# A fused attention and two-layer MLP kernel: a weight load moved, a gate pair put first in the operand work, and result buffers placed first in their pool

## The chip, the cores and the metric

The kernel runs on one core of one Trainium2 chip. The metric is the device time of one execution in microseconds; the kernel before has a median of 1094.09 us over three runs. TensorE is called PE below, its weight loads PEld, VectorE DVE, ScalarE ACT, GpSimd POOL, and SyncE, which issues nearly all transfers, SP.

## The reference, cut to what matters

Three stages follow each other, all in float32. Chunked attention (windows of 32 queries, 16 left and 8 right neighbours, 8 memory keys) gives x of 3072 tokens by 512. Layer one is gated, layer two is a SiLU layer:

```
scores = scale * np.matmul(q_c, k_full.transpose(0, 1, 3, 2))
a = np.exp(scores - max);  a = a / (sum(a) + 1e-09)
x = a @ v_full                                  # 3072 x 512
x = (sigmoid(x @ w_gate) * (x @ w_val)) @ w_out   # d_ff 1536
h = x @ w_in                                    # d_ff 2048
out = (h * sigmoid(h)) @ w_out2
```

The inputs are float64 on the host and arrive as pairs of 32-bit words, so each weight is first rebuilt (`rebias` on ACT, `join` on DVE) and split into a high and a low part (`high` on ACT, `rest` on DVE). A product is then three matmuls: high by high, high by low, low by high.

## The kernel before, in words

**Prologue.** The first 512 tokens (four tiles, 0 to 3) go through attention before any layer work can start. The order of that work on all engines is written out by hand in the string `PROLOGUE` (L38): each word is a step and a tile or a weight unit. `sc`, `max`, `sub`, `exp`, `sum`, `nm` make the probabilities of a tile, `pt` transposes them on PE and copies them to SBUF on ACT, `px` multiplies by the values, `tr` transposes the result on DVE. `rebias.1`, `join.1`, `high.0`, `rest.0` are steps of weight units 0 (gate columns 0) and 1 (value columns 0). `idle` and `short` are filler matmuls on PE. `load.4` issues the weight loads up to unit 4; the first transfer that this call issues waits for the exp of tile 3 (`behind`, L507). Loads issued before it are those of L472 to L484: queries and keys, then values, with gate unit 0 ahead of the last value tile and, by `feed1.load(2)` at L484, value unit 1 at the end. SP issues transfers strictly in this order.

**Layer one.** Four blocks of 512 tokens (block one to four) run directly: for each of 12 column tiles f, PE computes gate (`pg`) and value (`pv`), ACT the sigmoid (`sg`), DVE the product, and PE the output product `y` of the f before. Attention of later tiles is laid between (`run_events`, L601): `sx` on PE reads `at`, the copy of the transposed probabilities that ACT makes. From block two on, a planner (`Pace`, L803) spends the spare DVE and ACT time on operand work: it forms sums of weight quarters, for the products of the last third of layer one (`PairC`, kinds g, v and o) and of layer two (`Pair2`, two 128-column units of the raw weight `in_w2i_dram`, loaded by SP into `stg_w2i`). The list `items` (L1274 to L1277) gives its order: pair 0 of layer two's first weight, then gate pair 0 and value pair 0, and so on. The constructor of `Pace` issues the load of the first `Pair2` and makes the sums `tcg` of the first gate pair on DVE (`ahead`). Results go through five result buffers (`co`) to DRAM; the engines' instruction order is exactly the order in which the planner emits.

**The rest.** The last 1024 tokens of layer one (b = -1) and layer two (b = 0 to 2, 1024 tokens each) use seven products of summed quarters in place of eight (`pair2`, `out2`). During b = -1 and most of b = 0 a second `Pace` prepares the second weight of layer two in the pool `pp` (L1351): tags `stg0` and `stg1` (4 KB per partition each), `f` (8 KB) and four result buffers `co0` to `co3` (4 KB each, stored to `w2o_d`). After pair 5 of b = 0 the planner finishes, `pp` is closed, and the pool `p3` (L1368) takes its place; `g2_of` (L1046) puts the four activation tiles `g3..` of column pairs 6 and 7 there (16 KB). Tags get their addresses in the order in which they are first used, so in the kernel before `co0` to `co3` are the last 16 KB of `pp`, and `p3`'s four tiles lie on them.

Of the kernel before, what the change touches and what calls it, by code (L numbers as in the profile page):

```python
# [10 lines left out]
I32 = mybir.dt.int32  # L11
# [4 lines left out]
P = 128  # L16
# [21 lines left out]
PROLOGUE = """  # L38
idle.1 short.1 half.0 spread.1 hx.0 half.1 short.1 hx.1 sum.0 spread.2 spread.3 sc.1 nm.0 max.1 sub.1 exp.1 sc.2 max.2 sub.2
exp.2 sc.3 sum.1 nm.1 pt.0 max.3 sub.3 exp.3 load.4 qk.4 idle.1 px.0 sum.2 nm.2 pt.1 rebias.0 sum.3 nm.3  # L40
idle.1 px.1 tr.0 pt.2 pt.3 v.4 tr.1 join.0 rebias.1 px.2 tr.2 px.3 idle.1 high.0 tr.3 rest.0 join.1
"""
NP = 0
NRING = 5
# [12 lines left out]
def moe_kernel(ctx: ExitStack, tc: tile.TileContext, qh, kh, vh, wg, wv, wo, w2i, w2o, out):  # L57
# [15 lines left out]
    def w_slot(i, name):  # L73

        return main.tile([P, 2, 2, 512], F32R, tag=f"w{i}", name=name)
# [121 lines left out]
    def att_load_v(t, vb):  # L197
        nc.sync.dma_start(out=vb, in_=vh[t])
        v_t[t] = vb
# [188 lines left out]
    with tc.manual_schedule():  # L388
# [83 lines left out]
        feed1 = Feed(units)  # L472
# [7 lines left out]
        for t in range(n0):  # L480
            if t == n0 - 1:
                feed1.load(LV)
            att_load_v(t, vs[t])
        feed1.load(2)  # L484

        warm = ps_m("warm")
        fill = ident.rearrange("p (o n) -> p o n", o=1).to_broadcast([P, 4, P])
# [494 lines left out]
        for b in range(-1, NB2):  # L982
            base[b] = len(granules)
            if b < 0:
# [4 lines left out]
                for i in ORDER2:  # L989
                    for q in range(NPAIRC // 2):  # L990
                        if i in (S1, S2, S3, S4):
                            outs.append(wco_d[(S1, S2, S3, S4).index(i), q])
                        else:
                            f, c = 4 * q + (i != A11), 256 * (i == A22)
# [8 lines left out]
        def next_granule():  # L1003
            n = loaded[0]
            loaded[0] += 1
            if n >= len(granules):
                return
            w = w_slot(7 + n % NRING, f"wr{n}").rearrange("p a b c -> p (a b c)")
            k, src, *a = granules[n]
            if k == "o" or k == "m":  # L1010
                w = w.rearrange("p (b a m c) -> p b a m c", b=2, a=2, m=2)
                if k == "o":
                    nc.sync.dma_start(out=w.bitcast(F32), in_=src)
                else:
                    for j, part in enumerate(src):
                        nc.sync.dma_start(out=w[:, j].bitcast(F32), in_=part)
            else:
                w = w.rearrange("p (a m c) -> p a m c", a=2, m=4)
                src = wc_d[src[0], src[1]] if k == "c" else w2i_d[src]
                nc.sync.dma_start(  # L1020
                    out=w[:, :, : a[1]].bitcast(F32), in_=src[:, a[0], :, : a[1]]
                )
            ring[n] = w
# [248 lines left out]

        pending, rests = None, []
        items, gv, prep = [], [(k, p) for p in range(NPAIRC) for k in "gv"], None  # L1274
        for n in range(NPAIR):
            items.append(Pair2("i", n, p1))
            items += [PairC(*gv.pop(0)) for _ in range(2 - n % 2)]  # L1277
        seen = {}
        xgen = None
        for bi, n in enumerate(BLOCKS1[:NB1]):  # L1280
# [70 lines left out]
        pp_cm = tc.tile_pool(name="pp", bufs=1, side="right")  # L1351
        pool = pp_cm.__enter__()
        next_granule()
        prep = Pace([Pair2("o", p, pool) for p in range(NPAIR)], ["co0", "co1", "co2", "co3"], 1, 2.8)
        xgen = iter(())
        for b in range(-1, NB2):
# [106 lines left out]
```

## Time and profile before

| What | Value |
|---|---|
| Median of three runs | 1094.09 us (1093.42 to 1096.15) |
| Profiled execution, its own time | 1096.56 us |
| Its span, first to last instruction | 1094.7 us |
| PE busy | 1081.7 us (99% of the span) |
| DVE, ACT, POOL busy | 756.9 us, 531.5 us, 98.8 us |
| Granted TensorE clock | 1.00 |
| Chain that ended last | PE 96%, DMA 2%, ACT 1%, DVE 1% |

The profile's rows give times from the start of the span in microseconds. "Idle before" is the time that an engine stood still ahead of a group of instructions, with an arrow to what ended it. An engine name with a q (SPq) is its sequencer, which issues transfers and waits. "issue" as a releaser means that the engine waited for nothing that the profile shows. Line numbers are those of the kernel before; in the changed kernel everything after L484 stands one line higher.

### The profile page before, as it was taken

The numbers are of one execution on the slowest core, as the hardware profiler recorded it, in microseconds if no ns is written. First come the engines' busy times: TensorE is split into PE (matmuls) and PEld (weight loads), VectorE is DVE, ScalarE is ACT, GpSimd is POOL, SyncE is SP. The second block draws the span as 40 slices with busy tenths as digits, with TensorE's granted clock in tenths as the row PEclk, the third lists the DMA queues.
The fourth block names the chain that finished last, engine by engine and source line by source line (L and its number), as shares of the span: only waits on it lengthen the run. The fifth ranks groups of instructions, "written<-read, shape, count | busy, mean of one in ns | idle before, by whom it ended". The sixth has DMA issues, their size and how long they took to land.

```text
span 1094.7 us, 18989 instructions
## 1 busy us (share of the span) xinstructions
PE 1081.7 (99%) x7584; PEld 887.8 (81%) x7584; DVE 756.9 (69%) x1133; ACT 531.5 (49%) x775; POOL 98.8 (9%) x76
## 2 busy tenths in 40 slices
PE   7999999999999999999999999999999999999998
PEld 4888878888888888888888888788888888888887
DVE  7898867777767666657779966469634489443665
ACT  5766545455535453443345555455344445344542
POOL 1000001000000101011111011110011010011000
PEclk9999999999999999999999999999999999999999
DMA  8878787889878787689999599775665756656651
GB/s 332 277 272 291 283 285 255 298 304 310 296 275 292 272 289 281 227 281 343 344 339 352 177 295 361 270 274 207 230 202 202 282 195 224 210 187 208 218 215 67
DMA packets 106391, 288.02 MB, mean 263 GB/s; under 512 B 8640, under 2 KB 39616, under 8 KB 95552
## 3 DMA queue, kind: packets, MB, share of 16 engines
q1 hardware_dynamic: 105872, 286.30, 74.8%
q8 instruction: 60, 0.98, 0.4%
q10 hardware_dynamic: 432, 0.52, 0.1%
q14 instruction: 27, 0.22, 0.1%
HBM read 210.24 MB, written 76.55 MB: 262 GB/s over the span
## 4 chain that ended last, share of the span: by engine, by line
PE 96%; DMA 2%; ACT 1%; DVE 1%; issue 0%; SPq 0%; DVEq 0%; ACTq 0%
PE o L1244 21%; PE c L1071 20%; PE pv L360 12%; PE pg L360 11%; PE y L103 4%; PE y L107 4%; PE y L105 4%; PE sx L303 1%; PE sx L219 1%; PE o_-1_1_6458 L1244 1%; PE o_-1_0_6457 L1244 1%; PE pt L287 1%; DMA stg_w2i<-in_w2i_dram 1%; PE c_-1_4v L1071 1%; PE c_-1_2v L1071 1%; PE c_-1_5v L1071 1%
## 5 line engine op out<-in xcount | busy, mean ns | idle before, releaser
L1071 PE MATMUL c<-xp,wr 128*128 128x512 f32 x1008 | 229.3, 389 | 0.9 <-ACT s L1107 0.9
L1244 PE MATMUL o<-gf,wr 128*128 128x512 f32 x1008 | 229.0, 389 | 0.0
L1071 PEld LDWEIGHTS c<-xp,wr 128*128 128x128 f32 x1008 | 189.1, 188 | 40.6 <-ACT s L1107 1.4
L1244 PEld LDWEIGHTS o<-gf,wr 128*128 128x128 f32 x1008 | 189.2, 188 | 39.3
L360 PE MATMUL pv<-x,w 128*128 128x512 f32 x564 | 138.2, 394 | 0.0
L360 PE MATMUL pg<-x,w 128*128 128x512 f32 x564 | 138.1, 394 | 0.0
L1179 DVE TENSOR_TENSOR gf<-g,gf 128x1024 fp32r<-128x1024 f32 x84 | 103.8, 1239 | 46.4 <-ACT gf L1175 45.9
L1175 ACT CAST gf<-g 128x1024 fp32r<-128x1024 f32 x84 | 88.1, 1052 | 86.8 <-PE o L1244 71.2
L360 PEld LDWEIGHTS pv<-x,w 128*128 128x128 f32 x564 | 104.2, 188 | 22.9 <-DVE sg L375 0.2
L360 PEld LDWEIGHTS pg<-x,w 128*128 128x128 f32 x564 | 104.4, 188 | 21.7 <-ACT w L143 0.2
L1036 DVE TENSOR_TENSOR s<-c,s 128x512 f32<-128x512 f32 x48 | 33.1, 690 | 57.2 <-PE c L1071 57.2
L1112 POOL TENSOR_TENSOR s<-s,s 128x512 f32<-128x512 f32 x24 | 34.5, 1436 | 322.6 <-ACT s L1111 322.6
L1039 DVE TENSOR_TENSOR g<-g,g 128x1024 f32<-128x1024 f32 x48 | 58.8, 1224 | 0.0
L377 ACT CAST g<-sg 128x512 fp32r<-128x512 f32 x48 | 29.7, 620 | 54.3 <-DVE sg L375 54.1
L380 DVE TENSOR_TENSOR g<-sg,g 128x512 fp32r<-128x512 f32 x48 | 35.1, 732 | 28.9 <-ACT g L377 28.9
L1042 ACT ACTIVATE g<-s 128x512 f32<-128x512 f32 x48 | 30.3, 631 | 48.1 <-DVE s L1036 48.1
L370 ACT ACTIVATE sg<-pg 128x512 f32<-128x512 f32 x48 | 28.6, 596 | 51.3 <-PE pg L360 45.1
L1036 DVE TENSOR_TENSOR u<-c,s 128x512 f32<-128x512 f32 x24 | 16.6, 690 | 50.1 <-PE c L1071 44.0
L312 DVE STREAM_TRANSPOSE x<-sx 128x512 f32<-128x512 f32 x20 | 14.3, 716 | 39.2 <-PE sx L219 36.1
L673 POOL TENSOR_TENSOR tcv<-w 128x512 f32<-128x512 f32 x12 | 16.2, 1371 | 268.2 <-DVE fcg L636 268.2
L375 DVE TENSOR_TENSOR sg<-pv,sg 128x512 f32<-128x512 f32 x48 | 32.9, 685 | 9.1 <-PE pv L360 5.4
L268 ACT ACT_TABLE_LOAD x20 | 25.7, 1283 | 26.8 <-DVE e L260 26.7
(606 smaller groups left out, 1623.9 us busy)
## 6 DMA issues: line engine op xcount, KB each, us to landing
wr<-w2o_d SPq DMA_DIRECT2D x42, 1024.0 KB, 4.8
wr<-w2i_d SPq DMA_DIRECT2D x24, 1024.0 KB, 5.4
wor<-wo_d SPq DMA_DIRECT2D x36, 512.0 KB, 6.8
wr<-w2i_d SPq DMA_DIRECT2D x24, 768.0 KB, 4.5
w2o_d<-coo SPq DMA_DIRECT2D x56, 256.0 KB, 7.0
w2i_d<-coi SPq DMA_DIRECT2D x24, 512.0 KB, 7.3
wr<-wc_d SPq DMA_DIRECT2D x12, 1024.0 KB, 7.2
v<-in_vh_dram SPq DMA_DIRECT2D x21, 512.0 KB, 5.6
```

Source lines behind the costliest of these rows:

```text
L103: nc.tensor.matmul(o, w_hi, x_hi, start=first, stop=False)
L105: nc.tensor.matmul(o, w_hi, x_lo, start=False, stop=False)
L107: nc.tensor.matmul(o, w_lo, x_hi, start=False, stop=last)
L360: nc.tensor.matmul(o[:, :n], w[:, pw, kt * P : (kt + 1) * P], x[kt][:, px, :n], start=i == 0, stop=i == len(steps) - 1,)
L380: nc.vector.tensor_tensor(out=g[:, 1, :n], in0=sg[:, :n], in1=g[:, 0, :n].bitcast(F32), op=ALU.subtract)
L1036: nc.vector.tensor_tensor(out=o, in0=a, in1=b_, op=ALU.add)
L1039: nc.vector.tensor_tensor(out=o, in0=a, in1=b_, op=ALU.subtract)
L1071: nc.tensor.matmul(o, w[:, pw, m, kt * P : (kt + 1) * P], X[i][:, px, kt], start=first and j == 0, stop=j == 5, skip_group_check=not first,)
L1112: nc.gpsimd.tensor_tensor(out=s5, in0=s5, in1=s1, op=ALU.add)
L1175: nc.scalar.copy(f[:, 0], src)
L1179: nc.vector.tensor_tensor(out=f[:, 1], in0=src, in1=f[:, 0].bitcast(F32), op=ALU.subtract)
L1244: nc.tensor.matmul(c[at[i], dp], w[:, pw, pl, dp * P : (dp + 1) * P], f[:, px, pl], start=i in (A11, S1, S2) and pp == 0 and j == 0, stop= ...
```

## The change

Three edits. First, `feed1.load(2)` goes, so that the load of value unit 1 is issued by `load.4`, as the first of three transfers there, and in `PROLOGUE` the step `high.0` moves ahead of `px.3` and `tr.2`, and `rebias.1` behind the `idle` that follows `px.3`. Second, `items` begins with gate pair 0, and the other pairs are dealt so that the total stays eight `Pair2` and twelve `PairC`. Third, four tiles with the tags `co0` to `co3` are taken from `pp` before its planner exists; nothing reads or writes them, they only make these tags the first 16 KB of the pool.

```
@@ PROLOGUE
-idle.1 px.1 tr.0 pt.2 pt.3 v.4 tr.1 join.0 rebias.1 px.2 tr.2 px.3 idle.1 high.0 tr.3 rest.0 join.1
+idle.1 px.1 tr.0 pt.2 pt.3 v.4 tr.1 join.0 px.2 high.0 tr.2 px.3 idle.1 rebias.1 tr.3 rest.0 join.1
@@ moe_kernel
             if t == n0 - 1:
                 feed1.load(LV)
             att_load_v(t, vs[t])
-        feed1.load(2)
...
         items, gv, prep = [], [(k, p) for p in range(NPAIRC) for k in "gv"], None
+        items.append(PairC(*gv.pop(0)))
         for n in range(NPAIR):
             items.append(Pair2("i", n, p1))
-            items += [PairC(*gv.pop(0)) for _ in range(2 - n % 2)]
+            items += [PairC(*gv.pop(0)) for _ in range(1 + (n % 2 == 0 and n > 0))]
...
         pool = pp_cm.__enter__()
         next_granule()
+        for j in range(4):
+            pool.tile([P, 512, 2], I32, tag=f"co{j}", name=f"co{j}")
         prep = Pace([Pair2("o", p, pool) for p in range(NPAIR)], ["co0", "co1", "co2", "co3"], 1, 2.8)
```

**Place one: SP in the prologue.** The five transfers around the value unit's load, before, with the semaphores that each issue waits for (`stg_wg`, `stg_wv`: raw gate and value weight units; `kv_96`: buffer of tile 3, here its values):

```order
L118 DMA stg_wg_126<-in_wg_dram 128x1024 [waits DMAHW5_49]
L198 DMA kv_96<-in_vh_dram 128x1024 [waits DMAHW6_49]
L118 DMA stg_wv_129<-in_wv_dram 128x1024 [waits DMAHW7_49]
L118 DMA stg_wg_266<-in_wg_dram 128x1024 [waits DMAHW0_49,Activation_49]
L118 DMA stg_wv_268<-in_wv_dram 128x1024 [waits DMAHW1_49]
```

And in the changed kernel:

```order
L118 DMA stg_wg_126<-in_wg_dram 128x1024 [waits DMAHW5_49]
L198 DMA kv_96<-in_vh_dram 128x1024 [waits DMAHW6_49]
L118 DMA stg_wv_264<-in_wv_dram 128x1024 [waits DMAHW7_49,Activation_49]
L118 DMA stg_wg_266<-in_wg_dram 128x1024 [waits DMAHW0_49]
L118 DMA stg_wv_268<-in_wv_dram 128x1024 [waits DMAHW1_49]
```

The order of the transfers is the same; only the wait for ACT (the exp) moves one transfer forward, onto the value unit's load.

**Place two: ACT at the start of block two.** From the sigmoid of column tile 0 to the copy `at` that PE's next attention step reads, before (`stg_w2i`: raw units of pair 0; `y`: outputs of block one):

```order
L370 ACTIVATE sg_0_1744<-pg_0_1731 128x512
L123 ACTIVATE stg_w2i_1721<-stg_w2i_1721 128x512
L123 ACTIVATE stg_w2i_1723<-stg_w2i_1723 128x512
L377 CAST g_0_1767<-sg_0_1744 128x512
L919 COPY y_0_0_1784<-y_0_594 128x512
L919 COPY y_0_2_1790<-y_2_596 128x512
L288 COPY at_1797<-pt_1796 128x512
L783 CAST coi_0_1811<-fi_1761 128x512
L783 CAST coi_1_1813<-fi_1761 128x512
```

And in the changed kernel (`ccg`: result buffers of gate pair 0, from the sums `fcg`):

```order
L370 ACTIVATE sg_0_1744<-pg_0_1731 128x512
L713 CAST ccg_0_1757<-fcg_1746 128x512
L713 CAST ccg_1_1759<-fcg_1746 128x512
L377 CAST g_0_1776<-sg_0_1744 128x512
L918 COPY y_0_0_1793<-y_0_594 128x512
L918 COPY y_0_2_1799<-y_2_596 128x512
L288 COPY at_1806<-pt_1805 128x512
L123 ACTIVATE stg_w2i_1721<-stg_w2i_1721 128x512
L123 ACTIVATE stg_w2i_1723<-stg_w2i_1723 128x512
```

The two instructions that read the freshly loaded raw weight now stand behind the copy `at`, and two casts of the gate pair's sums stand in their old place. On DVE the four sums of gate pair 0 and one low part stand where the two joins stood.

**Place three: ACT at pair 6 of b = 0,** where the first activation tile of `p3` is written, before, with the semaphores waited for:

```order
L1107 COPY s_0_6_7363<-c_0_6_7360 128x512 [waits PE_49,Activation_49]
L1111 COPY s_0_6_7364<-c_0_6_7362 128x512 [waits PE_49,Activation_49]
L1175 CAST gf_2_7389<-g_2_11_7236 128x1024 [waits Activation_49]
L1042 ACTIVATE g_3_11_7397<-c_0_6_7360 128x512 [waits DMAHW3_49,DMAHW2_49,DMAHW4_49,DMAHW1_49,DMAHW5_49,DMAHW0_49,DMAHW7_49,PE_49,Activation_49]
L1042 ACTIVATE g_3_22_7409<-s_0_6_7364 128x512 [waits DVE_49]
```

And in the changed kernel:

```order
L1106 COPY s_0_6_7367<-c_0_6_7364 128x512 [waits PE_49,Activation_49]
L1110 COPY s_0_6_7368<-c_0_6_7366 128x512 [waits PE_49,Activation_49]
L1174 CAST gf_2_7393<-g_2_11_7240 128x1024 [waits Activation_49]
L1041 ACTIVATE g_3_11_7401<-c_0_6_7364 128x512 [waits DMAHW3_49,DMAHW2_49,DMAHW4_49,DMAHW1_49,DMAHW5_49,DMAHW0_49,DMAHW7_49,PE_49,Activation_49]
L1041 ACTIVATE g_3_22_7413<-s_0_6_7368 128x512 [waits DVE_49]
```

The rows are the same but for numbers: the first write into `p3` names the same seven transfer semaphores in both.

## Rows read from the trace of the kernel before

**Rows 1.** Page, part 1: busy time, share and instructions of each engine

```profile
PE 1081.7 (99%) x7584; PEld 887.8 (81%) x7584; DVE 756.9 (69%) x1133; ACT 531.5 (49%) x775; POOL 98.8 (9%) x76
```

**Rows 2.** Waits of PE, 30 us to the end: total, times, longest

```profile
PE sx L303 <- ACT at L288: 1.5, 1, 1.5
PE c L1071 <- ACT s L1107: 0.9, 1, 0.9
```

**Rows 3.** Timeline of PE, 134 to 144 us: start, us, instruction [idle before]

```profile
137.05 0.60 PE L287 MATMUL pt<-ident,e 128*128 128x128 f32 x4
137.41 3.02 PE L360 MATMUL pg<-x,w 128*128 128x512 f32 x12
141.91 0.86 PE L303 MATMUL sx<-v,at 64*32 64x64 f32 x64 [1.49 <-ACT at L288]
```

**Rows 4.** Timeline of ACT, 131 to 142 us

```profile
131.80 0.60 ACT L370 ACTIVATE sg<-pg 128x512 f32<-128x512 f32 x1 [0.70 <-PE pg L360]
135.31 0.69 ACT L123 ACTIVATE stg_w2i<-stg_w2i 128x512 f32<-128x512 f32 x1 [2.92 <-DMA stg_w2i<-in_w2i_dram]
137.67 0.69 ACT L123 ACTIVATE stg_w2i<-stg_w2i 128x512 f32<-128x512 f32 x1 [1.67 <-DMA stg_w2i<-in_w2i_dram]
139.78 0.62 ACT L377 CAST g<-sg 128x512 fp32r<-128x512 f32 x1 [1.42 <-DVE sg L375]
140.31 1.06 ACT L919 COPY y<-y 128x512 f32<-128x512 f32 x2
141.26 0.60 ACT L288 COPY at<-pt 128x512 f32<-128x512 f32 x1
```

**Rows 5.** Timeline of DVE, 110 to 160 us

```profile
131.69 1.28 DVE L673 TENSOR_TENSOR tcg<-w 128x512 f32<-128x512 f32 x2
...
139.01 0.69 DVE L375 TENSOR_TENSOR sg<-pv,sg 128x512 f32<-128x512 f32 x1
...
142.24 1.54 DVE L636 TENSOR_TENSOR fi<-fi 128x256 f32<-128x256 f32 x4
```

**Rows 6.** Timeline of PE, 0 to 42 us: the prologue's end

```profile
14.86 0.35 PE L303 MATMUL px<-v,at 64*32 64x64 f32 x17 [0.75 <-issue]
...
20.80 1.18 PE L303 MATMUL px<-kv,at 64*32 64x64 f32 x97 [1.64 <-issue]
...
23.43 2.30 PE L347 MATMUL pg<-x,w 128*128 128x512 f32 x8 [0.40 <-ACT x L564]
```

**Rows 7.** Timeline of ACT, 0 to 42 us

```profile
19.38 0.67 ACT L123 ACTIVATE stg_wv<-stg_wv 128x512 f32<-128x512 f32 x1 [0.23 <-DMA stg_wv<-in_wv_dram]
19.93 0.61 ACT L143 CAST w<-t_wg 128x512 fp32r<-128x512 f32 x1
22.76 2.18 ACT L564 CAST x<-x 128x512 fp32r<-128x512 f32 x4 [2.22 <-DVE x L312]
```

**Rows 8.** Timeline of SP, 6.8 to 16 us: transfers issued

```profile
7.62 0.37 SPq L198 DMA_DIRECT2D kv<-in_vh_dram  x1
8.91 0.33 SPq L118 DMA_DIRECT2D stg_wv<-in_wv_dram  x1
14.78 0.33 SPq L118 DMA_DIRECT2D stg_wg<-in_wg_dram  x1
```

**Rows 9.** Transfers issued at 7.62, 8.91 and 14.78: KB, us to landing

```profile
kv<-in_vh_dram SPq DMA_DIRECT2D x1, 512.0 KB, 10.5
stg_wv<-in_wv_dram SPq DMA_DIRECT2D x1, 512.0 KB, 10.4
stg_wg<-in_wg_dram SPq DMA_DIRECT2D x1, 512.0 KB, 5.8
```

**Rows 10.** DMA queues, 18 to 19.3 us: packets, MB, share of 16 engines

```profile
q1 hardware_dynamic: 139, 0.50, 97.8%
q8 instruction: 1, 0.02, 4.9%
```

**Rows 11.** Timeline of ACT, 672 to 712 us

```profile
701.77 0.60 ACT L1042 ACTIVATE g<-c 128x512 f32<-128x512 f32 x1 [7.51 <-DMA w2o_d<-coo]
```

More of the change, by code (lines that the diff above doesn't have):

```diff
@@ L40 @@
 exp.2 sc.3 sum.1 nm.1 pt.0 max.3 sub.3 exp.3 load.4 qk.4 idle.1 px.0 sum.2 nm.2 pt.1 rebias.0 sum.3 nm.3
-idle.1 px.1 tr.0 pt.2 pt.3 v.4 tr.1 join.0 rebias.1 px.2 tr.2 px.3 idle.1 high.0 tr.3 rest.0 join.1
+idle.1 px.1 tr.0 pt.2 pt.3 v.4 tr.1 join.0 px.2 high.0 tr.2 px.3 idle.1 rebias.1 tr.3 rest.0 join.1
 """
@@ L483, in moe_kernel @@
             att_load_v(t, vs[t])
-        feed1.load(2)
         warm = ps_m("warm")
@@ L1274, in moe_kernel @@
         items, gv, prep = [], [(k, p) for p in range(NPAIRC) for k in "gv"], None
+        items.append(PairC(*gv.pop(0)))
         for n in range(NPAIR):
             items.append(Pair2("i", n, p1))
-            items += [PairC(*gv.pop(0)) for _ in range(2 - n % 2)]
+            items += [PairC(*gv.pop(0)) for _ in range(1 + (n % 2 == 0 and n > 0))]
         seen = {}
@@ L1353, in moe_kernel @@
         next_granule()
+        for j in range(4):
+            pool.tile([P, 512, 2], I32, tag=f"co{j}", name=f"co{j}")
         prep = Pace([Pair2("o", p, pool) for p in range(NPAIR)], ["co0", "co1", "co2", "co3"], 1, 2.8)
```

## The prediction

> **What bounds the kernel now.** I read the page's busy times first, then the waits of PE, then the stretch around each wait on every engine.
>
> PE is busy 1081.7 us of a span of 1094.7 [rows 1], so about 13 us of the span are not PE work, and most of these lie in the prologue, before the first weight product at 23.43 us [rows 6], and in the last stores. From 30 us to the end PE waits just twice: 1.5 us for the copy `at`, and 0.9 us for the copy `s` [rows 2]. An edit that only moves work of ACT, DVE or SP can give back no more than a PE wait that it removes. So the question for each of the three edits is which PE wait it touches, and the most that the two later ones can give is 1.49 + 0.94, some 2.4 us or 0.22%. A measurement of this kernel can tell about 0.3%, 3.28 us, from no change.
>
> The sum is made against the profiled execution, 1096.56 us with 1.86 us outside its span. That run is 2.47 us above the median of 1094.09 and just above the slowest of the three timed runs; the difference that I work out I then take from the median.
>
> **Block two: the wait for `at`.** On PE the transposes of 137.05 are followed by the gate product, and the next attention step starts at 141.91 after 1.49 us idle, so the gate product ended at 140.42 [rows 3]. ACT makes the copy at 141.26 for 0.60 us, to 141.86, though its input was there at about 137.65 (137.05 + 0.60) [rows 3, 4]. ACT was late because it takes instructions in order and two of them, ahead of the copy, waited for the raw weight of pair 0: 2.92 us and 1.67 us idle. DVE stood behind the same loads, so that its product `sg` came at 139.01 and ACT's cast `g` behind that at 139.78 [rows 4, 5].
>
> After the change no transfer is waited for between the sigmoid and the copy (place two). I work the new order out from rows. DVE ends the sums `tcg` at 131.69 + 1.28 = 132.97; four sums take 1.54 as a group, to 134.51 [rows 5]. Two casts on ACT at 0.62 each (the cast at 139.78 has this size) end at 135.75 [rows 4]; DVE's low part, 0.69 like `sg`, starts after the first cast and ends near 135.8, then the product `sg` at 0.69 ends at 136.5. The cast `g` ends at 137.1, the two `y` copies (1.06) wait for PE's output product, which ends at 137.05, and end at 138.2; the copy `at` ends at 138.8 [rows 3 to 5]. PE needs it at 140.42. The wait of **1.49 us** goes with 1.6 us to spare, and what hides the gate pair's work is exactly the time in which ACT and DVE stood still.
>
> What is late next? The two reads of the raw weight, now behind the copy, start near 138.8; the second load landed before 137.67 [rows 4], so they run. Two more stores of original gate and value quarters go to SP behind these loads; they don't delay the loads, and everything behind them (`wor`, `y` stores, the next tile) lands a little later. The next ACT instruction that could wait for this is the next sigmoid, whose `sg` buffer needs the first `y` store. PE needs that sigmoid only at the following gate product, after the attention step, the value product and the output product, each of the last two about as long as the gate product (137.41 to 140.42), so some 7 us later. In the other direction, all later operand work of blocks two to four is emitted in another order, with the same planner rules; in the old order, among some twenty such items, PE never waited after 142 us [rows 2]. I take 0 for the rest. Bounds of the whole edit: −1.49 (the wait gone, nothing new) to 0 (a wait of the same size elsewhere, since the one that the trace shows is the only one of its kind).
>
> **Prologue: the value unit's load.** Before, it was issued at 8.91 and took 10.4 us; the transfer issued before it, at 7.62, took 10.5; the next one, issued at 14.78, took 5.8 [rows 8, 9]. They land at 18.1, 19.3 and 20.6: 1.3 us apart and in the order of issue, while the time from issue to landing halves. So the load sat behind a queue for most of its 10.4 us. Issued at 14.78, it still stands behind the values of tile 3, which land at 18.1, and lands at about 19.4, at the latest where the transfer issued at 14.78 landed before, 20.6. The transfers behind it keep their places. On ACT `rebias.1` waited for the load until 19.38, and the next thing that matters, the cast of x, came at 22.76 after 2.22 us idle, which DVE's transposes ended [rows 7]. Landing as late as 20.6, `rebias.1` ends at 21.3, still 1.5 us before that cast. `high.0` (0.61 us) now runs ahead of it in time that ACT has to spare. Value taken: **0**.
>
> The bounds need the row that sets the prologue's end. PE stops for 0.75 us and for 1.64 us in the middle of a run of equal `px` matmuls, each time with the releaser "issue" [rows 6]: no semaphore, no tile. Between 18 and 19.3 us, in the second stop's first part, the profile has one packet of the instruction queue q8 beside 139 of the loads, which fill 97.8% of the 16 DMA engines [rows 10]. I read the stops as PE out of instructions while its refill shares the DMA engines with the loads. If a shorter load queue let the refill through at once, the edit would give up to −1.64. At the other end, if the load took 10.4 us again from 14.78, it would land at 25.2 and `rebias.1` would hold the cast of x until 25.85, +3.1. The nearest row, the transfer issued at the same instant, says neither.
>
> A rule of the Trainium skill bears on the first of these ends. Its page "DMA: Bandwidth & Descriptors", section "Queues, rings and completion order", says that each DMA engine takes turns between the queues that have work, a packet at a time, so that a refill waits for the packet ahead of it and not for the depth of the load queue. By that rule the edit gives 0 here, since the load queue is never empty between 8.9 and 18 us in either order; by the other reading it gives −1.64. No row of this trace separates the two.
>
> **The g tiles.** ACT stands still for 7.51 us before the first `g` of pair 6, until the last store of the result buffers has landed, and starts at 701.77 [rows 11]; PE pays 0.9 us of that [rows 2]. With `co0` to `co3` first in the pool, `p3`'s four tiles lie on `stg0`, `stg1` and `f`, read long before, so by address nothing would hold them. But in the changed kernel the same ACT row names the same seven transfer semaphores as before (place three), and the last seven transfers of that pool are the stores of these buffers. The wait belongs to the closing of the pool as a whole and not to a tile's address. So the edit doesn't do what its name says: **0**, bounds −0.94 to 0, and the row of the order puts it at 0. The four tiles that nobody writes issue nothing.
>
> **The sum.** 0 − 1.49 + 0 = −1.49, for the profiled execution 1095.07, from the median 1094.09 − 1.49 = **1092.6 us**, a gain of 0.14%.
>
> **The rivals.**
> - *The refill is freed as well.* −1.49 − 1.64 = −3.13, 1090.96. For it: the stop sits in a stretch where the loads fill the DMA engines. Against it: the same bytes are moved over the same time, and the load is already issued again when the stop begins at 19.2. Chance 0.11.
> - *The g tiles come free.* −1.49 − 0.94 = −2.43, 1091.66. Against it stands the row of semaphores. Chance 0.04.
> - *A new wait takes the old one's place.* Pair 0's fourth cast now reuses the buffer of gate pair 0's first result, and so waits for that store; it stands ahead of the next copy `at` on ACT, and so do casts of later pairs. If one store lands 2 us or more after I reckon, PE waits again. Price up to 1.49, total 0, 1094.1. Against it: the planner leaves a buffer alone for three steps after its store is issued, and in the old order no such cast made PE wait. Chance 0.14.
> - *Slower: the value unit's load lands late.* It is the only load issued after the exp that the start of layer one needs. It decides from a landing after 22.1 (22.76 − 0.67), 7.3 us after its issue; at 10.4 us it costs 3.1, total +1.6, 1095.7. If block two also gives nothing, 1097.2. Against it: the transfer issued at that instant took 5.8. Chance 0.07.
>
> **How the numbers follow.** The forecast has 0.64, the rivals 0.36 together. The runs before lie from 0.67 below to 2.06 above their median. The range goes from the freed refill with 0.6 for run spread, 1090.4, to no gain with 1.3 for it, 1095.4; left out are the late load and the tails. Faster by over 0.3% means under 1090.81: half of the first rival, some of the second and the lower tail of the forecast, 0.11. Slower by over 0.3% means above 1097.37: the worse end of the last rival and something that I haven't seen, 0.05. Within 0.3%: 0.84.
>
> **What would show it.** Block two: no wait of PE for ACT L288 near 140 us, `ccg` casts where `stg_w2i` stood, and the first read of `stg_w2i` on ACT with no idle before it. Prologue: the load issued near 14.8, landing near 19.4, the two stops "issue" of 0.75 and 1.64 much as before, the first weight product near 23.4. The g tiles: ACT idle some 7.5 us again before the first `g` of pair 6, and PE's 0.9 us again. The prediction is wrong if the first weight product moves by a microsecond or more, if PE has a wait for ACT or DVE after 142 us that it hadn't, or if ACT's 7.5 us have gone.

## The result and the profile after

| What | Before | After |
|---|---|---|
| Median, six runs of each side by side | 1094.34 us (1093.42 to 1096.15) | 1100.25 us (1099.39 to 1101.77) |
| Ratio, 95% interval | | 1.0054 (1.0041 to 1.0067) |
| Profiled execution, its span | 1096.56, 1094.7 us | 1100.11, 1098.2 us |
| PE, DVE, ACT, POOL busy | 1081.7, 756.9, 531.5, 98.8 us | 1082.6, 768.0, 529.8, 101.4 us |

The change made the kernel 0.54% slower, 5.9 us by the medians, where 1092.6 us were forecast and a range up to 1095.4. The profiled executions differ by only 3.5 us, since the one of before was an unusually long one (second experiment below).

The view of what PE waited for, from 30 us to the end, after (line waited for, us in total, times, longest):

```profile
PE sx L303 <- ACT at L288: 5.8, 6, 1.6
PE c L1070 <- ACT s L1106: 1.2, 1, 1.2
```

It answers to [rows 2]: one wait of 1.5 us for the copy `at` has become 5.8 us in six, and a seventh of 0.13 us is too short for this list. The wait in pair 6 has stayed. PE's timeline shows five of the six (start, duration, engine, line, operation, in brackets the idle time before it and what ended it; the sixth stands further down):

```profile
175.93 0.37 PE L303 MATMUL sx<-v,at 64*32 64x64 f32 x20 [0.23 <-ACT at L288]
...
213.67 0.34 PE L303 MATMUL sx<-v,at 64*32 64x64 f32 x15 [0.72 <-ACT at L288]
...
325.88 0.33 PE L303 MATMUL sx<-v,at 64*32 64x64 f32 x13 [1.00 <-ACT at L288]
...
345.52 0.29 PE L303 MATMUL sx<-v,at 64*32 64x64 f32 x8 [1.05 <-ACT at L288]
...
383.92 0.30 PE L303 MATMUL sx<-v,at 64*32 64x64 f32 x9 [1.14 <-ACT at L288]
```

None is near 142 us, where [rows 3] had the wait that the forecast took away. ACT's timeline there, after, answers to [rows 4]: the two casts of the gate pair stand where ACT had waited for the raw weight, and the copy is made at 137.12 rather than 141.26 (1.7 us of this are the earlier start of layer one in this execution).

```profile
130.19 0.60 ACT L370 ACTIVATE sg<-pg 128x512 f32<-128x512 f32 x1 [0.70 <-PE pg L360]
132.59 1.15 ACT L713 CAST ccg<-fcg 128x512 fp32r<-128x512 f32 x2 [1.80 <-DVE fcg L635]
135.64 0.62 ACT L377 CAST g<-sg 128x512 fp32r<-128x512 f32 x1 [1.90 <-DVE sg L375]
136.16 1.07 ACT L918 COPY y<-y 128x512 f32<-128x512 f32 x2
137.12 0.60 ACT L288 COPY at<-pt 128x512 f32<-128x512 f32 x1
137.60 1.24 ACT L123 ACTIVATE stg_w2i<-stg_w2i 128x512 f32<-128x512 f32 x2
```

So the forecast's step happened, and seven waits came elsewhere. At each of them ACT's cast `g` ahead of the copy had waited for DVE's product `sg`. The last one, at 422.58, shows how. DVE's timeline, after, from the end of an attention normalisation (`e<-e,r`) to the product `sg`:

```profile
411.22 0.69 DVE L282 TENSOR_TENSOR e<-e,r 128x512 f32<-128x512 f32 x1
411.83 1.28 DVE L643 TENSOR_TENSOR ccv<-fcv,ccv 128x512 fp32r<-128x512 f32 x2
413.22 0.42 DVE L635 TENSOR_TENSOR fcg<-tcg 128x256 f32<-128x256 f32 x1
...
415.00 3.46 DVE L643 TENSOR_TENSOR ccg<-fcg,ccg 128x512 fp32r<-128x512 f32 x2 [0.23 <-ACT ccg L713]
418.38 0.42 DVE L133 TENSOR_SCALAR stg_w2i<-stg_w2i 128x512 int32<-128x512 int32 x1
...
420.65 0.68 DVE L375 TENSOR_TENSOR sg<-pv,sg 128x512 f32<-128x512 f32 x1
```

ACT behind it, and then PE, in the same execution:

```profile
421.43 0.62 ACT L377 CAST g<-sg 128x512 fp32r<-128x512 f32 x1 [2.90 <-DVE sg L375]
421.95 0.58 ACT L288 COPY at<-pt 128x512 f32<-128x512 f32 x1
```

```profile
417.58 0.60 PE L287 MATMUL pt<-ident,e 128*128 128x128 f32 x4
417.93 3.02 PE L360 MATMUL pg<-x,w 128*128 128x512 f32 x12
422.58 0.86 PE L303 MATMUL sx<-v,at 64*32 64x64 f32 x64 [1.64 <-ACT at L288]
```

DVE does 8.8 us of operand work (411.83 to 420.65), with no pause over 0.23 us: low parts of one item, all sums of the next and its low parts, then the joins of a raw weight. The product `sg` comes behind that. ACT stands still for 2.90 us for it, and the copy `at`, whose input PE had finished at 418.2 (417.58 + 0.60), stands behind the cast `g` in ACT's order.

A second profiled execution of the kernel before (an experiment below) has the same tile with less work between. DVE, then ACT, then PE:

```profile
408.46 0.69 DVE L282 TENSOR_TENSOR e<-e,r 128x512 f32<-128x512 f32 x1
409.07 1.29 DVE L644 TENSOR_TENSOR ccv<-fcv,ccv 128x512 fp32r<-128x512 f32 x2
...
411.93 0.68 DVE L375 TENSOR_TENSOR sg<-pv,sg 128x512 f32<-128x512 f32 x1
```

```profile
412.70 0.62 ACT L377 CAST g<-sg 128x512 fp32r<-128x512 f32 x1 [3.88 <-DVE sg L375]
413.66 0.59 ACT L288 COPY at<-pt 128x512 f32<-128x512 f32 x1 [0.34 <-PE pt L287]
```

```profile
416.27 0.86 PE L303 MATMUL sx<-v,at 64*32 64x64 f32 x64
```

Here `sg` starts 2.8 us behind the normalisation's end (409.15) and the copy is made when PE's transposes end. In after `sg` starts 8.7 us behind the normalisation's end (411.91).

**Where the work comes from.** The two lists differ only by the swap of the first two items, so the sequence behind them is the same. What differs is when the planner emits it. It gets 2.15 us in each third of a column tile's step, less 2.1 where attention scores are met and less 1.75 where a normalisation stands, and it saves what it doesn't spend, up to 3.2 us. While it waits for a free result buffer it saves; when the buffer comes free it spends the savings in whichever step that happens. The table is worked out from the code alone: the planner's own costs of all that it emits in the step of a normalisation and in the two behind it, up to `sg` (in brackets the normalisation's step alone), with PE's wait at the attention step that follows, from the traces. Steps are counted in thirds of a column tile from the start of layer one.

| Normalisation's step | Before | After, wait | One step later, wait | Before, seven steps later, wait |
|---|---|---|---|---|
| 41 | 0.80 (0) | 4.10 (0.7) | 3.45 (1.15) | 0 |
| 47 | 0.80 (0) | 6.70 (3.0), **0.23** | 3.00 (0) | 4.10 (1.4) |
| 53 | 0.70 (0) | 4.10 (2.5) | 3.30 (0) | 6.00 (3.0), **0.90** |
| 59 | 3.00 (0) | 6.70 (3.0), **0.72** | 3.00 (0) | 6.70 (3.0), **1.19** |
| 65 | 3.30 (0) | 4.10 (2.5) | 3.30 (0) | 4.10 (2.5) |
| 71 | 3.00 (0) | 6.00 (3.0), **0.13** | 3.00 (0.8) | 5.55 (3.0), **0.87** |
| 77 | 5.30 (0) | 6.00 (2.55) | 2.55 (0) | 4.10 (2.5) |
| 83 | 3.40 (2.6) | 3.35 (0.8) | 3.40 (0) | 6.70 (3.0), **1.18** |
| 89 | 5.30 (2.55) | 4.10 (0.7) | 4.50 (0) | 4.10 (2.5) |
| 95 | 0.80 (0.8) | 6.00 (3.0), **1.00** | 3.40 (2.6) | 6.70 (3.0), **1.70** |
| 101 | 0.80 (0) | 6.70 (3.0), **1.05** | 3.00 (0) | 4.10 (2.5) |
| 107 | 3.45 (0) | 4.10 (1.4) | 3.45 (0), **0.57** | 6.00 (3.0), **2.32** |
| 113 | 3.80 (0.8) | 6.70 (3.0), **1.14** | 3.80 (0.8), **0.74** | 6.70 (3.0), **1.09** |
| 119 | 3.45 (0) | 4.10 (2.5) | 3.45 (0) | 4.10 (2.5) |
| 125 | 3.00 (0) | 6.70 (3.0), **1.64** | 3.00 (0) | 6.00 (2.55) |

In after PE waits at exactly the seven tiles where 3.0 us are booked in the normalisation's own step, and in the last column too. The sum over three steps alone doesn't part them: it is 6.00 at step 77 as well, where PE doesn't wait, with 2.55 of it in the normalisation's own step. The last two columns are experiments.

### The profile page after: what moved, and what is told of

Read it like the earlier page. It is cut to its first block, busy times and chain, and to the rows that moved or that the text cites. A ratio compares the mean times of both kernels' runs of the same rounds, so it can differ in the third digit from the quotient of the medians.

```text
span 1098.2 us, 19007 instructions
## 1 busy us (share of the span) xinstructions
PE 1082.6 (99%) x7584; PEld 888.4 (81%) x7584; DVE 768.0 (70%) x1133; ACT 529.8 (48%) x775; POOL 101.4 (9%) x76
## 4 chain that ended last, share of the span: by engine, by line
PE 87%; DVE 5%; ACT 3%; DMA 2%; issue 2%; SPq 0%; POOL 0%; DVEq 0%; ACTq 0%; POOLq 0%
PE o L1243 21%; PE c L1070 20%; PE pv L360 9%; PE pg L360 8%; PE y L103 3%; PE y L107 3%; PE y L105 3%; PE sx L303 1%; PE o_-1_1_6462 L1243 1%; PE o_-1_0_6461 L1243 1%; PE sx L219 1%; PE c_-1_4v L1070 1%; PE c_-1_2v L1070 1%; PE c_-1_5v L1070 1%; PE c_-1_5g L1070 1%
## 5 line engine op out<-in xcount | busy, mean ns | idle before, releaser
L360 PEld LDWEIGHTS pg<-x,w 128*128 128x128 f32 x564 | 104.4, 188 | 21.6 <-ACT w L143 0.3
L375 DVE TENSOR_TENSOR sg<-pv,sg 128x512 f32<-128x512 f32 x48 | 32.9, 686 | 12.4 <-PE pv L360 11.1
L107 PE MATMUL y<-g,wor 128*128 128x512 f32 x144 | 38.7, 390 | 0.0
## 6 DMA issues: line engine op xcount, KB each, us to landing
wr<-w2i_d SPq DMA_DIRECT2D x24, 768.0 KB, 4.5
```

The source lines that it names most:

```text
L107: nc.tensor.matmul(o, w_lo, x_hi, start=False, stop=last)
L360: nc.tensor.matmul(o[:, :n], w[:, pw, kt * P : (kt + 1) * P], x[kt][:, px, :n], start=i == 0, stop=i == len(steps) - 1,)
```

## The experiments

**Which edit does it.** Three kernels are the kernel before with one edit each. The prologue's edit alone:

```
 PROLOGUE
-... join.0 rebias.1 px.2 tr.2 px.3 idle.1 high.0 tr.3 rest.0 join.1
+... join.0 px.2 high.0 tr.2 px.3 idle.1 rebias.1 tr.3 rest.0 join.1
-        feed1.load(2)
```

> The kernel before with the prologue's edit alone (the value unit's load behind the fourth tile's exp, and the new order of its steps). In the profile of after, the first weight product of layer one starts 1.70 us earlier than in that of before, and PE's two stops without a releaser (0.75 and 1.64 us) are gone. Theory 1: the stops are in every execution of before, and the edit removes them: about 1.7 us less than before, no wait for the copy at behind 142 us. Theory 2: the stops belong mostly to the one profiled execution of before, which was 2.2 us above its own median: the timed difference is 0 to -0.5 us, whatever the profile shows. Theory 3: the edit costs something in timed runs that the profile hides, since after lost 5.9 us by its timed runs and 3.5 by its profiled one: +1 to +2.5 us.

Measured: 1093.92 us against 1093.93, ratio 0.9995 (0.9986 to 1.0004), so between -1.5 and +0.4 us; its profile still has two stops without a releaser (0.87 and 0.92 us). The list's edit alone:

```
+        items.append(PairC(*gv.pop(0)))
         for n in range(NPAIR):
             items.append(Pair2("i", n, p1))
-            items += [PairC(*gv.pop(0)) for _ in range(2 - n % 2)]
+            items += [PairC(*gv.pop(0)) for _ in range(1 + (n % 2 == 0 and n > 0))]
```

> The kernel before with the edit of the operand list alone (gate pair 0 ahead of pair 0). Theory 1 (the new list shifts the planner's phase, so that six microseconds of planned operand work stand between an attention normalisation and the product sg, and the copy at comes late): block two's wait of 1.49 us goes, seven others of 5.9 us together come, so about +4.4 us against before, DVE busy about 768 us, and the waits at the same seven tiles as in after. Rival (the waits come from the traffic of the other two edits, or from where the prologue leaves the queues): less than +1.5 us and fewer than three waits.

Measured: 1100.65 us against 1093.93, ratio 1.0058 (1.0046 to 1.0071), +6.7 us. DVE is busy 766.6 us, and PE's waits for `at` stand at the tiles of after:

```profile
PE sx L303 <- ACT at L288: 5.7, 6, 1.6
```

The loss belongs to this edit whole. It is above the +4.4 that I expected, since the 1.49 us that I credited aren't there to be won (next experiment). The third edit alone:

```
+        for j in range(4):
+            pool.tile([P, 512, 2], I32, tag=f"co{j}", name=f"co{j}")
         prep = Pace([Pair2("o", ...
```

> The kernel before with the third edit alone (four tiles that nobody writes, ahead of the others in the operand pool). Theory 1 (the wait belongs to the closing of the pool, wherever the g tiles lie): PE's wait in pair 6 stays at 0.7 to 1.2 us, time within 0.5 us of before. Rival (the edit does what it says): the wait goes, about 0.9 us less.

Measured: 1093.84 against 1094.09, ratio 0.9997 (0.9988 to 1.0006); PE's wait in pair 6 is still 0.7 us. No difference, as forecast.

**Is the wait of 1.49 us in every execution of before?** The kernel before, unchanged.

> The kernel before, unchanged, profiled a second time. The prologue's edit alone showed no wait for the copy at in block two, though it leaves that place as it was, and took as long as before by its timed runs. Theory 1 (the wait of 1.49 us belongs to some executions of before only: it hangs on when two raw loads land, and the profiled execution of before was 2.6 us above the median): the second profile shows no such wait, or one under 0.5 us, and a time near 1094. Rival (the wait is in every execution of before, and the prologue's edit took it away while it cost as much elsewhere): the wait is there again, 1.3 to 1.6 us.

Measured: 1093.38 us, span 1091.5. PE has no wait for `at`. ACT's timeline, which answers to [rows 4]:

```profile
132.76 0.69 ACT L123 ACTIVATE stg_w2i<-stg_w2i 128x512 f32<-128x512 f32 x1 [1.85 <-DMA stg_w2i<-in_w2i_dram]
134.09 0.69 ACT L123 ACTIVATE stg_w2i<-stg_w2i 128x512 f32<-128x512 f32 x1 [0.64 <-DMA stg_w2i<-in_w2i_dram]
...
137.67 0.60 ACT L288 COPY at<-pt 128x512 f32<-128x512 f32 x1
```

The same two waits for the raw weight are 1.85 and 0.64 us, where [rows 4] has 2.92 and 1.67, and the copy comes in time. The kernel with the prologue's edit alone and the one with the third edit alone show no wait there either; a fifth execution (before with another pool, below) shows 0.48 us. So the wait of 1.49 us hung on when two loads landed in one execution.

**Does the phase decide, or the list?** The changed kernel, with its own list, and the planner's first call left out:

```
-                        prep.go(us - sum(DVE_US.get(w, 0) for w in names))
+                        if it + i >= 37:
+                            prep.go(us - sum(DVE_US.get(w, 0) for w in names))
```

> The changed kernel with its own list and rules; only the planner's first call, at the first step of block two, is left out, so that all operand work starts one step (about 3 us) later. By the planner's arithmetic the work between an attention normalisation and the product sg is then nowhere more than 4.5 us, where after has 6.0 to 6.7 at the seven tiles whose copy at PE waited for. Theory 1 (the phase decides, not the list): no wait for the copy at, 1093 to 1094.5 us. Rival (the list with the gate pair first, or the amount of work, decides): waits of 3 us or more in sum, 1098 us or more.

Measured: 1096.86 us against 1093.7, ratio 1.0025 (1.0014 to 1.0036). Of 5.9 us of waits 1.3 are left: 0.57 at 362.24 (step 107), at a tile that had none in after, and 0.74 at 381.53 (step 113), at one that had 1.14. Six of the seven are gone and the seventh is smaller, with the same list, so the list by itself isn't the cause. But the time is over 2 us above what I expected, and the table marks neither of the two waits: it doesn't see the turn from one block to the next, where DVE also splits x and copies `y`. The trace shows part of what is late there. The first gate product of the new block, here and in the kernel with the prologue's edit alone:

```profile
348.99 3.60 PE L360 MATMUL pg<-x,w 128*128 128x512 f32 x12
```

```profile
349.99 2.88 PE L360 MATMUL pg<-x,w 128*128 128x512 f32 x12
```

Here DVE makes the low parts of x, which the last four of these matmuls read, only behind a join that had waited 1.86 us for ACT:

```profile
349.55 2.49 DVE L335 TENSOR_TENSOR x<-x,x 128x512 fp32r<-128x512 f32 x4
```

In the other kernel they start at 346.45, before the product. The value product follows the start of the gate product by 3.71 us here (352.70) and by 2.72 there (352.71), so PE loses another 1.0 us in pauses too short for the list of waits. What the rest of the difference to my expectation is stays open.

The other way round, before with its own list and seven calls left out (`it + i >= 43`):

> The kernel before, its list and prologue untouched; the planner's first seven calls in block two are left out. By its arithmetic 6.0 to 6.7 us of work, 3.0 of it in the step of the normalisation itself, then stand between the normalisation and sg ahead of the attention steps 57, 63, 87, 99, 111 and 117 (counted in thirds of a feature step from the start), and at most 5.6 elsewhere but for step 129 (6.0, 2.55 of it in that step). Theory 1 (phase): PE gets waits for the copy at there, and mostly there alone, 3 to 6 us in sum, so +3 to +6 us against before, with a list that had none. Rival (the wait comes with the new list): no wait, within 1.5 us of before.

Measured: 1111.44 us against 1093.7, ratio 1.0158 (1.0144 to 1.0171), +17.7 us. PE's waits and the timeline rows of the two largest:

```profile
PE sx L303 <- ACT at L288: 9.2, 7, 2.3
PE c_-1_0g L1071 <- DVE sg L375: 2.0, 1, 2.0
```

```profile
331.52 0.29 PE L303 MATMUL sx<-v,at 64*32 64x64 f32 x8 [1.70 <-ACT at L288]
...
370.88 0.26 PE L303 MATMUL sx<-v,at 64*32 64x64 f32 x4 [2.32 <-ACT at L288]
...
372.51 4.33 PE L360 MATMUL pv<-x,w 128*128 128x512 f32 x12
...
382.12 2.88 PE L360 MATMUL pv<-x,w 128*128 128x512 f32 x12
```

All six places named beforehand have the wait, and a seventh (5.55 us booked, 3.0 in the normalisation's step) that I had put below the line. A list behind which PE never waited for `sg` makes it do so seven times when it is started at another step. The size was missed: 9.2 us of these waits where I expected 3 to 6, work left over at the end of layer one, and a lower clock behind the longest waits (last section).

**Is it the burst in the normalisation's step?** The changed kernel, no operand work in such a step:

```
-                        prep.go(us - sum(DVE_US.get(w, 0) for w in names))
+                        prep.go(0.0 if "norm" in names else us - sum(DVE_US.get(w, 0) for w in names))
```

> The changed kernel, where the planner issues no operand work in a step that holds an attention normalisation (it goes to the steps behind it; all work is still done). Between the normalisation and sg there are then at most 4.1 us of planned work, where seven tiles had 6.0 to 6.7. Theory 1 (the burst makes sg, and by it the copy at, late): PE's seven waits go or shrink to under 1 us in sum, about 5 us less than after, some 1095 us or less. Rival (DVE has more work in all, or is slowed by GpSimd or by DMA traffic, wherever the work stands): the waits move to other tiles, their sum stays above 3 us and the time within 2 us of after's.

Measured: 1093.62 us against 1093.93, ratio 0.9993 (0.9984 to 1.0002). From 30 us to the end PE has this wait alone, and none for `at`, though DVE is still busy 762.5 us:

```profile
PE c L1070 <- ACT s L1106: 1.0, 1, 1.0
```

The whole loss is undone with the same list and the same work.

**Does ACT's order pass it on?** The changed kernel, the cast `g` and DVE's low part of it behind the copy `at` where a step has both:

```
+        if not late:
+            nc.scalar.copy(g[:, 0, :n], sg[:, :n])
         def lo():
+            if late:
+                nc.scalar.copy(g[:, 0, :n], sg[:, :n])
...
-                g_t[bi, f] = gated(sg, psv, n, f"{bi}_{f}", p1, 2, None if bi else rests)
+                turns = bi > 0 and "turn" in [w for w, t in events.get(it + 2, [])]
+                g_t[bi, f] = gated(sg, psv, n, f"{bi}_{f}", p1, 2, rests if turns else None if bi else rests, turns)
```

> The changed kernel, where in a step that ends with the copy at, ACT's cast g and DVE's low part of it are issued behind that copy, in place of ahead of it; the operand work stays as late on DVE as in after. The cast is needed by PE only in the following output product. Theory 1 (the wait is made by ACT's order: the copy stands behind a cast that waits for DVE's sg): PE's waits for at go, all but 0.5 us, about 5 us less than after. Rival (the copy is late by itself, since DVE's late work delays what PE transposes, or PE then waits for g instead): the sum of PE's waits between 150 and 440 us stays above 3 us.

Measured: 1095.74 us against 1093.93, ratio 1.0017 (1.0008 to 1.0026). Its waits of PE, but for the one in pair 6:

```profile
PE pg L360 <- ACT sg L370: 1.4, 2, 0.8
```

All waits for `at` are gone while DVE is as late as in after (769.0 us busy; at the last tile `sg` starts 8.7 us behind the normalisation's end again, at 417.68), so PE's waits came by way of ACT's order. 1.4 us turned up at two gate products instead.

**What share has GpSimd?** The changed kernel, zeros in place of GpSimd's sums:

```
-                self.whole(self.t[0], even, eng)
-                self.whole(self.t[1], odd, eng)
+                if eng is nc.gpsimd:
+                    for t in self.t:
+                        nc.gpsimd.memset(t, 0.0)
+                else: ...
```

> The changed kernel without GpSimd's sums of the next gate or value pair (two additions of 1.3 to 1.5 us each; their buffers are filled with zeros instead, so the operands of layer two's first stage lack them). In after seven low parts on DVE took 1.1 to 1.8 us where the others take 0.69, all seven while such a sum ran; four of them lie in the bursts ahead of two of PE's waits, 1.00 us at 325.88 and 1.64 at 422.58, none in the bursts ahead of the other five (0.23, 0.72, 0.13, 1.05, 1.14). Theory 1 (bursts first, GpSimd's slowing of DVE on top, 2.1 us in those two): those two waits go, the other five stay, 3.0 to 3.5 us left in sum, 2 to 3 us less than after. Rival a (the sums beside DVE are the whole cause): all seven go, 5 us or more less. Rival b (they cost PE nothing): the sum stays at 5.5 to 6 us.

Measured: 1096.47 us against 1094.09, ratio 1.0021 (1.0012 to 1.0030), so +2.4 where after has +5.9. Its waits of PE, but for the one in pair 6:

```profile
PE sx L303 <- ACT at L288: 1.9, 4, 0.7
PE y L103 <- issue: 1.3, 1, 1.3
```

No low part is longer than 0.70 us, and DVE is busy 754.8 us. Waits by place, after and here: 0.23 and 0.23, 0.72 and 0.72, 0.13 and 0.12, 1.00 and none, 1.05 and 0.23, 1.14 and none, 1.64 and 0.69. So the three before 300 us owe nothing to GpSimd, and the two that I had named shrink, though the later only by 0.95. Two more shrink that I had put down to the burst alone. For the one at 345.52 (1.05 to 0.23) the trace has a reason: GpSimd's sums slow more than low parts. Ahead of it DVE makes two sums of whole weights (`tc`), in after and here:

```profile
326.01 2.37 DVE L672 TENSOR_TENSOR tc<-wor 128x512 f32<-128x512 f32 x2
```

```profile
323.26 1.29 DVE L672 TENSOR_TENSOR tc<-wor 128x512 f32<-128x512 f32 x2
```

The attention work behind them (`e<-sx,m`) starts 3.74 us after PE's attention step in after (325.88 to 329.62) and 2.87 us after it here (324.23 to 327.10). The 0.87 us less are about what this wait lost, 0.82. For the one at 383.92 there are two reasons at hand: such a sum took 1.78 us at 361.17 in after, and here PE itself stopped for 1.32 us without a releaser, until 349.51, which gives the other engines as much time to catch up; I can't separate the two. By the timed runs GpSimd's sums account for some 3.5 of the 5.9 us, and only together with the burst: the kernel without operand work in normalisation steps has four slow low parts in layer one too, and loses nothing.

**The wait in pair 6.** In after ACT still stands still ahead of the first `g` of pair 6, as in [rows 11]:

```profile
705.30 0.60 ACT L1041 ACTIVATE g<-c 128x512 f32<-128x512 f32 x1 [7.74 <-DMA w2o_d<-coo]
```

Three kernels take these tiles from the pool `pp` itself, on the raw weights' and the sums' buffers, and leave it open:

```
-                pool = p2 if pp < NPAIRC // 2 else p3
-                g2[b, pp, r] = pool.tile([P, 2, 512], F32, tag=f"g{pp}{r}", name=...)
+                if pp < NPAIRC // 2:
+                    g2[b, pp, r] = p2.tile([P, 2, 512], F32, tag=f"g{pp}{r}", name=...)
+                elif r in ("11", "22"):
+                    tag = {"11": "stg0", "22": "stg1"}[r]
+                    g2[b, pp, r] = pool.tile([P, 2, 512], F32, tag=tag, name=...)
+                else:
+                    gw = pool.tile([P, 2, 2, 512], F32, tag="f", name=...)
+                    g2[b, pp, "12"], g2[b, pp, "21"] = gw[:, 0], gw[:, 1]
...
-                        pp_cm.__exit__(None, None, None)
-                        p3_cm = tc.tile_pool(name="p3", bufs=1, side="right")
-                        p3 = p3_cm.__enter__()
```

With the planner one step later (to be compared with that kernel alone, 1096.86):

> The last kernel but one (the changed kernel, planner one step later), where the four g tiles of the last two pairs are taken from the operand pool itself, on the buffers of the raw weights and of the sums, and the pool stays open to the end; nothing then waits for the pool's last stores. Theory 1 (PE's 0.9 us in pair 6 come from the closing of the pool as a whole): that wait of PE and ACT's 7 us ahead of the first g of pair 6 go, 0.9 us less than the kernel without it. Rival (something else is late there): PE waits 0.5 us or more at the same place for another engine.

Measured: 1095.36 us, ratio to before 1.0011 (1.0003 to 1.0020), 1.5 us less than without it; the wait is gone. On the kernel before:

> The kernel before with its last four g tiles of layer two on the operand pool's own buffers, the pool left open to the end. Theory 1 (the closing of the pool costs PE 0.8 to 0.9 us in pair 6): that wait goes, 0.8 to 0.9 us less than before. Rival: PE waits as long for something else there, no difference.

Measured: 1093.26 us against 1094.09, ratio 0.9993 (0.9984 to 1.0002), -0.8 us, the size of the wait, though the interval reaches zero. ACT no longer waits for a transfer there:

```profile
693.04 0.60 ACT L1042 ACTIVATE g<-c 128x512 f32<-128x512 f32 x1 [1.13 <-PE c L1077]
```

**The best of both.** The changed kernel with no operand work in normalisation steps and these tiles in the open pool:

> The changed kernel with no operand work in the steps of a normalisation, and layer two's last four g tiles on the operand pool's own buffers with the pool left open. Theory 1: no wait for the copy at and none in pair 6, 0.9 us less than the first of the two alone (1093.6), so some 1092.7 us, 0.1% less than before. Rival (other waits of a microsecond or more come up): 1093.5 or more.

Measured: 1092.21 us (1091.70 to 1093.70) against 1094.09, ratio 0.9981 (0.9973 to 0.9990). From 30 us to the end its trace has no wait of PE long enough for the list. It is faster than before by 1.9 us and than after by some 8 us.

## Why the prediction was wrong, step by step

- **What bounds the kernel.** Right as far as the changes could be traced: they were PE's waits (part of the +17.7 us, and of the loss with the planner one step later, isn't traced). DVE's busy time by itself isn't the price: without operand work in normalisation steps it is 762.5 us, 5.6 more than before, and nothing is lost.
- **Block two, -1.49.** The order worked out as reckoned: no transfer is waited for ahead of the copy, made at 137.12, against 138.2 by my sum. The sigmoid starts 1.6 us earlier in this execution, so the copy is 0.5 us later than I had it: the low part took 1.71 us at 133.24, where I took 0.69. But the gain isn't there. I took a wait of one execution off the median of others, and that execution was 2.47 us above that median; the wait was one of the reasons why. Four other executions with the old order at this place show 0, 0, 0 and 0.48 us.
- **"I take 0 for the rest", bounds -1.49 to 0.** This is the step that failed. It measured +6.7 us with the list's edit alone. The argument was that the same rules had never made PE wait among some twenty items. That was true of one phase of the planner, not of its rules: the same old list, started at another step, loses 17.7 us. I had the planner's costs and allowances in the code and could have added up, for the new list, what falls between a normalisation and `sg`; that sum is 6.0 or more at all seven tiles, and at one more where PE doesn't wait.
- **The rival "a new wait takes the old one's place".** The right direction and the right copy, with the wrong mechanism and size: no cast waited for the store of a result buffer; the casts waited for DVE's `sg`. Price 5.9 us in seven waits, where I allowed 1.49.
- **Prologue, 0.** Right within the timed interval (-1.5 to +0.4 us). The load was issued at 15.04 and landed at 19.32, where I had said 14.8 and 19.4. The profile of after has neither stop of [rows 6], all 128 `px` matmuls run in one piece:

```profile
18.66 1.60 PE L303 MATMUL px<-kv,at 64*32 64x64 f32 x128
...
21.73 0.50 PE L347 MATMUL pg<-x,w 128*128 128x512 f32 x1 [0.41 <-ACT x L563]
```

  By the forecast's own list of signs this speaks against it: the first weight product moved by 1.70 us, from 23.43. It looks like the rival of the freed refill, but the stops come and go. The nine stops in mid run that the fourteen executions show, eight in the prologue and the one at 349.51, end 1.3 to 1.6 us behind the end of a 16 KB packet of the instruction queue (before: a packet until 19.24, PE again at 20.80), which bears out the forecast's reading of them. Four of six executions with the old prologue have them there and one of eight with the new, and that one is the kernel with this edit alone. The first weight product starts between 21.43 and 23.43 us in six executions with the old prologue (mean 22.5) and between 21.23 and 22.66 in eight with the new (mean 21.6). The means differ by 0.9 us, inside the scatter of one execution, and the timed runs of the edit alone show no gain. Whether it brings the refill forward in most executions stays open. So the rule that the forecast cites from the Trainium skill's page "DMA: Bandwidth & Descriptors", section "Queues, rings and completion order", and from which it took that the edit gives 0, is neither borne out nor refuted.
- **The g tiles, 0.** Right, with the cause that I gave: the wait belongs to the closing of the pool, stays with the third edit alone (0.7 us), and goes when the pool isn't closed.
- **The range.** It left out, but for a chance of 0.05 of a loss over 0.3%, what a shifted schedule can cost, since I had bounded the rest of layer one by the waits that the old trace shows. The bound should have come from the slack: `at` is done 2.0 us before PE needs it in the second profile of before (from 414.25, which is 413.66 + 0.59, to 416.27), and a burst of three planned microseconds in the wrong step uses that up.

## What to carry to other kernels

When a planner emits work by a budget, a change to the head of its list shifts everything behind it: add up, from its own costs, what now falls ahead of each instruction that the busiest engine waits for, before taking "the same rules" for "the same waits". A budget that may be saved should not be spendable in the steps that are already full. And a wait that one profiled execution shows is worth its size only if other executions show it too: look first at how far that execution is from the median.

## What the runs showed of the hardware

**DVE and GpSimd take turns.** Single instructions of after, DVE first, then POOL:

```profile
415.00 1.75 DVE L643 TENSOR_TENSOR ccg<-fcg,ccg 128x512 fp32r<-128x512 f32 x1 [0.23 <-ACT ccg L713]
416.68 1.78 DVE L643 TENSOR_TENSOR ccg<-fcg,ccg 128x512 fp32r<-128x512 f32 x1
```

```profile
414.92 1.29 POOL L672 TENSOR_TENSOR tcv<-w 128x512 f32<-128x512 f32 x1 [15.38 <-DVE fcg L635]
416.17 1.74 POOL L672 TENSOR_TENSOR tcv<-w 128x512 f32<-128x512 f32 x1
```

POOL's first sum ends at 416.21, DVE's first low part 0.54 us later; POOL's second ends at 417.91, 1.16 us behind that, and DVE's second at 418.46, 0.55 us behind that. Alone, the low part takes 0.69 us and the sum 1.29. All seven slow low parts of after's layer one lie so, and without the sums there are none. The product `sg`, which reads PSUM, takes 0.68 us beside such a sum as well. The Trainium skill's page "SBUF — State Buffer", section "SBUF: two separate sides", says that the two engines share a pair of ports as a lock held for a whole instruction, by a DVE instruction with two inputs in SBUF among others, against a GpSimd instruction that reads SBUF. The trace agrees: 1.75 and 1.78 us where both have two inputs there, 0.68 where one of DVE's is in PSUM.

This is also where DVE's greater busy time in after comes from. In layer one thirteen of its instructions are slowed so (seven low parts of operands, five sums `tc`, one low part of `g`), by 13.2 us together over 0.69 each; in before three, by 2.0 us. That is 11.2 us more, and the busy times, 768.0 and 756.9, differ by 11.1: the work is the same, but the shifted planner puts more of it beside GpSimd's sums.

**A wait of PE can cost more than its length.** In before with the planner seven steps later, behind the wait of 2.32 us that ended at 370.88, the granted clock (PEclk, the column behind POOL) was lower for some 6 us, between its two levels of 1.2 and 2.4 GHz in the mean of each window:

```profile
371.00:374.00 3.00, 3.00 (x132) 2.54 (x129) 3.00 (x5) 0.00 (x0) 0.22 (x1) 0.65 0.37 89
374.00:377.00 3.00, 3.00 (x12) 2.40 (x11) 1.45 (x3) 0.00 (x0) 0.00 (x0) 0.78 0.98 349
377.00:380.00 3.00, 3.00 (x15) 2.49 (x14) 0.69 (x1) 2.84 (x4) 0.00 (x0) 1.00 1.06 378
```

The twelve value matmuls at 372.51 took 4.33 us, and those of the next column tile, at 382.12, 2.88. Behind the wait of 2.0 us for `sg` the clock was 0.57 from 474 to 478 us. Behind the wait of 1.70 us at 331.52 the clock stayed at 1.00, as it did behind after's longest, 1.64 us. So nothing shows that the seven waits of after cost more than their own length, 5.9 us, which is also what the timed runs lost. In the kernel with the longer ones the waits of the list come to 13.0 us, 0.7 of which before has too, against +17.7 us of time; not all of the rest is traced.
